# A gated mix of attention and ReLU-GLU on one core: new orders for the passes in the attention's rounds of three and four halves

## The chip, the cores and the metric

One core of one Trainium2 chip. The metric is device microseconds of one execution, the median of the runs shown. Below, "the profiled execution" is the one that left the trace.

## The reference, cut to what matters

x has 2048 rows (tokens) of 448 features. Two branches read it, and a gate of one number a token mixes them:

```
g = sigmoid((x * gate_w).sum(-1))
q, k, v = split(x @ wqkv)          # 16 heads of 28
p = softmax(q @ k.T * 28 ** -0.5)  # 2048 x 2048 a head
a = (p @ v) @ wo
gate, up = x @ W_gate, x @ W_up    # 1792 wide
h = gate * (gate > 0) * up
b = h @ W_down
out = g * a + (1 - g) * b
```

## The kernel before, in words

Everything is float32 outside. Where products need the precision, an operand is split in a high and a low float32r part, and a product is the sum of several passes: 11 matmuls (TERMS, L57) of 512 columns for one tile of q, k, gate or up.

A **first stage** (to about 125 us) makes q, k and v and starts on the attention. A **last stage** (from about 1090 us) is the output product and the down product of the other branch. Between them lie 32 **rounds**, and the change is in these. Each round works on eight key tiles of one head (128 keys against all 2048 queries), so a head takes two rounds. TensorE's order in a round is written out by hand, in a string with one letter for each piece of work (L43 to L48; the loop over the letters is L591 to L628):

- `s`, `scores` (L173): one matmul (L178) of a key tile against 512 queries, 114 rows deep, two of which bring in the queries' maxima. ScalarE takes its exp into P (L180). The result stands in one of **two** PSUM buffers `s` in turn, so a score must wait until the exp of the score two before it is done.
- `m`, `smax` (L144): two matmuls (L152) for the maxima of a head that comes later; VectorE reduces 128 x 1024 of them (L154). Two PSUM buffers `mx` in turn.
- `x`, `gu_mm` (L462): one of the 11 passes (L468) of one half, gate or up, of a tile of 128 of the other branch's hidden columns. When a gate half is full, ScalarE takes its relu (L481); after an up half VectorE multiplies (L484) and GpSimd sends the tile to HBM (L490). Two PSUM buffers `x` in turn.
- `h`: the last passes of the round's last two halves, 64 rows each, side by side.

After the string come the splits of the next weights (ScalarE L90, GpSimd L99) and `pv` (L496): 64 matmuls (L503) of P with V, which stand in one of the two `mx` buffers. Its result is copied by ScalarE (L507) after the first round of a head, and added by VectorE (L509) after the second.

Before the string `small_things` (L554) issues DMAs, and it does so again at the string's 17th `s`. In every second round, `smax_end` (L159) follows: TensorE transposes a head's maxima (L162), ScalarE copies them twice (L165, L166), VectorE subtracts (L96), and GpSimd sends two rows to Q (L169). Below a round is called odd when it begins with this, which also is when L507 stands ahead of it. Each engine works its instructions off in the program's order, so in an odd round the first exp of the string stands behind L507, L165 and L166 on ScalarE, and the first reduction behind the subtraction on VectorE.

Which strings run (L50, L52): FIRST once; then 28 rounds, of which 24 are LONG (three halves of gate and up) and four are WIDE (four halves; the 3rd, 6th, 9th and 18th of the 28); then LATE three times. Of the 28, the 1st, 3rd and so on are odd. A matmul of 512 columns is called a pass below: `s` and `x` are one, `m` is two.

A matmul is a weight load (PEld) and the stream (PE). A load runs beside the matmul ahead of it. The wait for a PSUM buffer is a wait of the load.

Of the kernel before, what the change touches and what calls it, by code (L numbers as in the profile page):

```python
# [41 lines left out]

FIRST = "s" * 12 + "mmlssxxxmsxsxuxmsxmsxsxmsxsxmsxsxmsxsxmsxsxmsxsxmsxsxmsx"  # L43

LONG = "mxsmsxxxxxsmsxsmsxxsmsxsmsxxsmxxsmsxsxxsmsxxsxsmxsxsmsxxsmsxsmsxxsmsxsxxsmsmxssh"
WIDE = "sxxmxmxxsxxmsxxsxsmxxssxmxmxsxxsxxsxsmsxxsmxssxxxsmsxxsxmsxmsxsxmsxsmxsxsxxsmsxxsmsmsxxsxsh"

LATE = "ssxxxssxxxssxxssxx" * 4 + "hh"  # L48

ROUNDS = [(FIRST, 2)] + ([(LONG, 3)] * 2 + [(WIDE, 4)]) * 2 + [(LONG, 3)] * 2  # L50

ROUNDS += ([(WIDE, 4)] + [(LONG, 3)] * 8) * 2 + [(LONG, 3)] * 2 + [(LATE, 4)] * 3  # L52
NP = 9
# [757 lines left out]
```

## Time and profile before

| | |
|---|---|
| median of 3 runs | 1297.71 us (1297.41 to 1298.08) |
| profiled execution, its own time | 1295.85 us |
| its span, first to last instruction | 1294.1 us |
| granted TensorE clock | 1.000 |
| busy: VectorE, ScalarE, GpSimd | 62%, 59%, 28% |
| first turned maxima in the 28 rounds | 166.2 us |
| first round of LATE | 1014.8 us |

In the profile a row of a timeline has the start, the length, the engine, the line of the kernel, what it writes and reads, and how many like it were merged; in brackets stand the idle time ahead of it and what ended that. The ends of matmuls are modelled; their starts are what can be compared. A row of the waits has who waited, for whom, the total in us, how often, and the longest.

### The profile page before, as it was taken

Reading aid. Unit: us, or ns where it says so; the run is one execution under the profiler, and the core shown is the slowest. Engines: PE = TensorE matmul, PEld = TensorE weight load, DVE = VectorE, ACT = ScalarE, POOL = GpSimd, SP = SyncE. Lnnn points to the kernel's source line nnn. Section 1 sums busy time; section 2 is a strip of 40 time slices with the busy share of each in tenths; the row PEclk is TensorE's granted clock in tenths of the full one; section 3 lists DMA queues with packets and bytes.
Section 4 is the critical chain, followed back from the end, with each engine's and each line's share of the span. In section 5 each row is a group of like instructions: output and inputs, shape, how many; then the busy total and the mean of one; then the engine's idle time right before and its main releaser. Section 6 shows DMA issues by size and latency. Waiting matters only on the chain.

```text
span 1294.1 us, 17710 instructions
## 1 busy us (share of the span) xinstructions
PE 1287.5 (99%) x6687; PEld 901.8 (70%) x6687; DVE 806.1 (62%) x834; ACT 767.0 (59%) x1402; POOL 365.8 (28%) x551
## 2 busy tenths in 40 slices
PE   9999999999999999999999999999999999999998
PEld 6888766666666666666666666666666656899997
DVE  6488766677677676777766667777777212663342
ACT  5212766666767677777776666767676865322121
POOL 3222132332313222222223332313132353641020
PEclk9999999999999999999999999999999999999999
DMA  9845524151426334141535142422341224644432
GB/s 322 284 162 229 155 75 103 60 124 55 117 63 182 76 81 96 52 103 45 139 108 119 50 111 66 109 69 79 71 142 38 82 91 142 198 136 148 134 110 78
DMA packets 53565, 148.87 MB, mean 115 GB/s; under 512 B 10024, under 2 KB 17128, under 8 KB 48872
## 3 DMA queue, kind: packets, MB, share of 16 engines
q1 hardware_dynamic: 36120, 98.34, 28.9%
q0 software_dynamic: 16928, 48.93, 10.5%
q8 instruction: 53, 0.87, 0.3%
q10 hardware_dynamic: 432, 0.46, 0.1%
q14 instruction: 32, 0.26, 0.1%
HBM read 102.06 MB, written 46.02 MB: 114 GB/s over the span
## 4 chain that ended last, share of the span: by engine, by line
PE 98%; ACT 0%; DMA 0%; SPq 0%; DVE 0%; issue 0%; ACTq 0%
PE gu L468 22%; PE sm L152 19%; PE po L503 17%; PE s L178 17%; PE acc L712 11%; PE qk L303 5%; PE v L321 3%; PE wo L668 3%; PE s L189 2%; DMA wr<-wq 0%; PE mt L162 0%; ACT WO L90 0%; SPq L253 0%; DVE W L96 0%; ACT V L191 0%
## 5 line engine op out<-in xcount | busy, mean ns | idle before, releaser
L154 DVE TENSOR_REDUCE mx<-sm 128x1 f32<-128x1024 f32 x512 | 614.4, 1221 | 106.1 <-PE sm L152 105.6
L180 ACT ACTIVATE P<-s 128x512 f32<-128x512 f32 x724 | 414.5, 597 | 161.8 <-PE s L178 123.0
L468 PE MATMUL gu<-X,wg 128*128 128x512 f32 (+1 forms) x1232 | 391.0, 400 | 0.2 <-ACT wg L90 0.2
L178 PE MATMUL s<-Q,K 114*128 114x512 f32 x932 | 367.6, 400 | 0.0
L152 PE MATMUL sm<-K,Q 112*128 112x512 f32 x1024 | 323.6, 397 | 0.0
L468 PEld LDWEIGHTS gu<-X,wg 128*128 128x128 f32 (+1 forms) x1232 | 226.6, 189 | 52.8 <-issue 8.8
L178 PEld LDWEIGHTS s<-Q,K 114*128 114x128 f32 x932 | 175.2, 188 | 88.9 <-ACT P L180 47.9
L152 PEld LDWEIGHTS sm<-K,Q 112*128 112x128 f32 x1024 | 192.1, 190 | 44.7 <-issue 10.1
L503 PE MATMUL po<-P,V 128*32 128x512 f32 x1600 | 181.0, 594 | 0.0
L490 POOL DMA_DIRECT2D h_d<-h x56 | 31.4, 560 | 518.7 <-DVE h L484 472.4
L99 POOL TENSOR_TENSOR wg<-wgr,wg 128x384 fp32r<-128x384 f32 x204 | 145.6, 731 | 8.1
L180 ACT ACTIVATE V<-s 128x512 f32<-128x512 f32 x208 | 119.5, 598 | 41.6 <-PE s L178 30.5
L712 PE MATMUL acc<-WD,hh 128*128 128x448 f32 x672 | 140.9, 368 | 0.0
L712 PEld LDWEIGHTS acc<-WD,hh 128*128 128x128 f32 x672 | 126.2, 188 | 12.8
L503 PEld LDWEIGHTS po<-P,V 128*32 128x32 f32 x1600 | 49.6, 110 | 111.2 <-issue 110.1
L90 ACT ACTIVATE hh<-hr 128x512 fp32r<-128x512 f32 x56 | 35.2, 631 | 119.3 <-PE acc L712 119.3
L96 DVE TENSOR_TENSOR hh<-hr,hh 128x512 fp32r<-128x512 f32 x56 | 46.1, 823 | 64.2 <-ACT hh L90 64.2
L303 PE MATMUL qk<-X,W 128*128 128x512 f32 x308 | 79.3, 398 | 0.3
L303 PEld LDWEIGHTS qk<-X,W 128*128 128x128 f32 x308 | 58.4, 190 | 14.9 <-ACT zt L326 0.5
L90 ACT ACTIVATE wg<-wgr 128x384 fp32r<-128x384 f32 x165 | 66.3, 491 | 2.3 <-PE gu L468 1.2
L509 DVE TENSOR_TENSOR os<-po,os 128x512 f32<-128x512 f32 x16 | 11.1, 691 | 88.8 <-PE po L503 88.8
L96 DVE TENSOR_TENSOR mh<-mr,mh 16x128 fp32r<-16x128 f32 x16 | 5.9, 366 | 91.3 <-ACT mh L166 91.3
(73 smaller groups left out, 756.6 us busy)
## 6 DMA issues: line engine op xcount, KB each, us to landing
wgr<-wgu SPq DMA_DIRECT2D x55, 512.0 KB
K<-qk_d SPq DMA_DIRECT2D x64, 224.0 KB
Q<-qk_d SPq DMA_DIRECT2D x64, 224.0 KB
h_d<-h POOLq DMA_DIRECT2D x56, 256.0 KB, 2.3
hr<-h_d SPq DMA_DIRECT2D x56, 256.0 KB
qk_d<-st POOLq DMA_DIRECT2D x21, 512.0 KB, 3.9
x_d<-X POOLq DMA_DIRECT2D x6, 1024.0 KB, 5.1
X<-x_d SPq DMA_DIRECT2D x24, 256.0 KB
```

The lines of the kernel that those rows point to most:

```text
L90: nc.scalar.activation(dst, src, AF.Copy)
L96: nc.vector.tensor_tensor(dst, src, f32(high), op=OP.subtract)
L99: nc.gpsimd.tensor_tensor(dst, src, f32(high), op=OP.subtract)
L152: nc.tensor.matmul(ps[:, c, :], Q[h][:GD, u * P:(u + 1) * P], K[h % 3][:GD, k0:k0 + TB], start=True, stop=True)
L154: nc.vector.tensor_reduce(MX[h][:, 2 * u + half:2 * u + half + 1], ps, axis=AX.XY, op=OP.max)
L178: nc.tensor.matmul(ps, K[h % 3][:GD + 2, kt * P:(kt + 1) * P], Q[h][:GD + 2, j * TB:(j + 1) * TB], start=True, stop=True)
L180: nc.scalar.activation(PT[i][:, j], ps, AF.Exp, scale=SCALE)
L303: nc.tensor.matmul(ps, W[:, a, c * P:(c + 1) * P], xf(tb, b), start=(n == 0), stop=(n == NT - 1))
L321: nc.tensor.matmul(ps[:, :VC], xf(tb, b)[:, t * P:(t + 1) * P], W[:, a, 2 * D:], start=(n == 0), stop=(n == NT - 1))
L468: nc.tensor.matmul(ps, WS[i][rows, s, a], xf(i // NF, b)[rows], start=(n == 0), stop=(n == NT - 1))
L503: nc.tensor.matmul(po[32 * j:32 * j + 32], V[:, h // 4 % 2, i % NK, h % 4], p[:, j], start=(i == i0), stop=(i == i0 + ni - 1))
L712: nc.tensor.matmul(ACC[i // NF][t][:, :D], HH[i][:, a, t * P:(t + 1) * P], WD[:, f, b], start=(f == 0 and n == 0), stop=(f == NF - 1 and n ...
```

## The change

The two strings LONG and WIDE are written anew. Both keep their letters: 32 `s`, 16 `m`, 31 `x` (WIDE: 42) and one `h`; only their order differs. The rest of the kernel is as it was.

```
-LONG = "mxsmsxxxxxsmsxsmsxxsmsxsmsxxsmxxsmsxsxxsmsxxsxsmxsxsmsxxsmsxsmsxxsmsxsxxsmsmxssh"
-WIDE = "sxxmxmxxsxxmsxxsxsmxxssxmxmxsxxsxxsxsmsxxsmxssxxxsmsxxsxmsxmsxsxmsxsmxsxsxxsmsxxsmsmsxxsxsh"
+LONG = "smsxmsxsxmsxsxmsxsmxsxsmxsxsxmsxsmxsxsxxxsmsmsxxsxmsxsxmsxsmxsxsmxsxsxmsxsmxxssh"
+WIDE = "xssmxxsxxsxxmssxmxsxxmssmxxsxsmxsxsmxsxsxxxxxxssmxxsxxmsxsmxsxsmxsxmsxsmxsxsmxsxxsmsxxsmxsh"
```

Counted in passes from the string's start, the first scores, the first maxima and the smallest distances are:

| | scores at | m at | smallest, score to next but one | smallest, m to next but one |
|---|---|---|---|---|
| LONG before | 3, 6, 12, 15, 17 | 0, 4, 13, 18 | 5 | 11 |
| LONG after | 0, 3, 7, 9, 13 | 1, 5, 11, 17 | 6 | 10 |
| WIDE before | 0, 10, 15, 18, 20 | 3, 6, 13, 21 | 5 | 9 |
| WIDE after | 1, 2, 7, 10, 15 | 3, 13, 18, 24 | 6 | 10 |

## The prediction

> **What bounds the kernel now.** I read the page first. TensorE works all the time and the chain that ended last runs through it.
>
> ```profile
> PE 1287.5 (99%) x6687; PEld 901.8 (70%) x6687; DVE 806.1 (62%) x834; ACT 767.0 (59%) x1402; POOL 365.8 (28%) x551
> ...
> PE 98%; ACT 0%; DMA 0%; SPq 0%; DVE 0%; issue 0%; ACTq 0%
> ```
>
> A busy PE may still place its matmuls further apart than it must. So the second view is the weight loads' waits between 166 and 1014.7 us, the 28 rounds whose orders change (24 LONG, 4 WIDE). A row gives the total us, the count and the longest wait.
>
> ```profile
> PEld s L178 <- ACT P L180: 47.4, 263, 0.2
> PEld s L178 <- ACT V L180: 13.8, 77, 0.2
> ...
> PEld po L503 <- DVE mx L154: 1.0, 4, 0.2
> ```
>
> The weights of a score wait 340 times for an exp; nothing waits for the maxima (m) except four short times at the products with V. Counting passes in the old strings (s and x one pass, m two) explains the number: in LONG 13 of the 30 scores with a score two before them in the round stand five passes behind it, in WIDE 7, and no score stands nearer. 24 x 13 + 4 x 7 = 340. Every five is late and no six is.
>
> The third view is the timeline inside one LONG round: start, length, engine.
>
> ```profile
> 446.15 0.40 PE L178 MATMUL s<-Q,K 114*128 114x512 f32 x1
> ...
> 446.58 2.49 ACT L180 ACTIVATE P<-s 128x512 f32<-128x512 f32 x4 [0.80 <-PE s L178]
> ...
> 446.86 0.39 PE L178 MATMUL s<-Q,K 114*128 114x512 f32 x1
> ...
> 447.09 0.39 PE L468 MATMUL gu<-X,wg 128*128 128x512 f32 x1
> 447.23 0.19 PEld L178 LDWEIGHTS s<-Q,K 114*128 114x128 f32 x1 [0.18 <-ACT P L180]
> 447.32 0.42 PE L178 MATMUL s<-Q,K 114*128 114x512 f32 x1
> ...
> 447.58 0.62 PE L152 MATMUL sm<-K,Q 112*128 112x512 f32 x2
> 447.94 0.19 PEld L178 LDWEIGHTS s<-Q,K 114*128 114x128 f32 x1 [0.17 <-ACT P L180]
> 448.04 0.40 PE L178 MATMUL s<-Q,K 114*128 114x512 f32 x1
> ...
> 448.28 0.62 PE L468 MATMUL gu<-X,wg 128*128 128x512 f32 x2
> ```
>
> Score at 446.15, exp at 446.58 (0.43 later), which lasts 0.60 and ends at 447.18; the load for the next score but one starts at 447.23, 0.05 later. So 1.08 us pass from a score to the load that it holds back, if ScalarE is free. The passes are 0.23 apart (446.86, 447.09, 447.32), and a load usually starts a whole pass ahead. This one starts 0.09 ahead; the next matmul comes 0.26 on, not 0.23. The load at 447.94 starts 0.10 ahead and costs 0.01. So some 0.10 ahead is free, what is missing is paid, and the idle 0.18 of a load costs about 0.03.
>
> Fourth, what all 340 cost. The mean lengths of the matmuls of these rounds, and the spread of the scores (shortest/median/longest):
>
> ```profile
> L178 PE MATMUL s<-Q,K 114*128 114x512 f32 x896 | 353.4, 400 | 0.0
> L468 PE MATMUL gu<-X,wg 128*128 128x512 f32 x912 | 304.7, 395 | 0.0
> L152 PE MATMUL sm<-K,Q 112*128 112x512 f32 x896 | 283.6, 398 | 0.0
> ...
> L178 PE MATMUL s<-Q,K x896: 389/396/501, 167.1 to 1007.0; 114*128 114x512 f32 x180
> ```
>
> A score's recorded length grows with the lateness (0.42 above, against 0.39). Mean less median is 4 ns, x 896 = 3.6 us. Against the gate-and-up matmuls it is 5 ns, 4.5 us.
>
> **The change part by part.** Nothing is added or taken out: each string keeps its 32 s, 16 m, its x and its h (31 x in LONG, 42 in WIDE), and with them all loads, splits and DMAs. Only places move. The DMAs that SP issues at the 17th score move by under five passes (1.2 us) in a round of 23 us; no transfer is waited for there in the rows of loads.
>
> *Removed.* In the new strings the smallest distance of a score to the next but one is six. Six passes are 1.39 us; the chain takes 1.08, so the load may start 0.31 ahead, where 0.10 is enough: 0.21 to spare. All 340 late loads should go. Counting: of a LONG's 13, some 7 cost 0.02 to 0.03 and three 0.01, about 0.18; 24 x 0.18 + 4 x 0.1 = 4.7 us. The means said 3.6 and 4.5. I take **4.6**; the ends are 3.6 and 5.2.
>
> Two scores two passes apart, which the new LONG has twelve times, queue on ScalarE. The nearest row is two scores one pass apart:
>
> ```profile
> 402.80 0.65 PE L178 MATMUL s<-Q,K 114*128 114x512 f32 x2
> ...
> 403.23 1.09 ACT L180 ACTIVATE P<-s 128x512 f32<-128x512 f32 x2 [0.33 <-PE s L178]
> ```
>
> Two exps end in 1.09, so the second starts 0.49 after the first. For scores at pass 0 and 2 the second exp starts at 0.92 instead of 0.89: 0.03 of the 0.21 to spare. A relu stands behind the 11th x, at pass 34, in about every second LONG; with it the exp of the score at pass 37 starts 0.10 late, and the load for pass 43 still starts 0.2 ahead. I cost both at nothing; a miss is a rival below.
>
> *Added.* The front of a round. In the odd rounds a head's maxima are turned by a transpose (14 in the window, in 12 LONG and 2 WIDE), and ScalarE and VectorE have three small pieces of work ahead of the first exp and the first maximum. The old WIDE begins with a score, as the new LONG does. Its front:
>
> ```profile
> L162 PE MATMUL mt<-ident,m 128*16 128x128 f32 x14 | 3.9, 277 | 0.0
> ...
> 410.81 0.28 PE L162 MATMUL mt<-ident,m 128*16 128x128 f32 x1
> 410.84 0.48 PE L178 MATMUL s<-Q,K 114*128 114x512 f32 x1
> 410.94 0.60 ACT L507 ACTIVATE os<-po 128x512 f32<-128x512 f32 x1 [3.89 <-PE po L503]
> 411.16 0.63 PE L468 MATMUL gu<-X,wg 128*128 128x512 f32 x2
> ...
> 411.44 0.25 ACT L165 ACTIVATE mr<-mt 16x128 f32<-16x128 f32 x1
> ...
> 411.72 0.31 ACT L166 ACTIVATE mh<-mr 16x128 fp32r<-16x128 f32 x1
> ...
> 411.94 0.57 ACT L180 ACTIVATE P<-s 128x512 f32<-128x512 f32 x1
> ```
>
> The first exp starts 1.13 after the transpose and ends at 1.70, though its score was ready at 0.5. There the old WIDE has its third score at pass 15, far off. The new strings have it at pass 7. Pass 1 is at 0.35, so pass 7 is at 0.35 + 6 x 0.233 = 1.75; the load is released at 1.70 + 0.05 = 1.75, just when the matmul should start. What that costs shows at the round's first matmul, whose load also starts with it: 410.84 to 411.16 is 0.32 where 0.23 is usual. **0.10 in each of 14 rounds.** The second exp follows 0.50 behind the first (410.94 to 411.44 for two that queue), ends at 2.23 and releases at 2.28. In the new LONG its score stands at pass 9, 2.21 + 0.10 = 2.31: the load starts 0.03 ahead where some 0.10 are needed to cost nothing, another **0.06 in 12 rounds**. In WIDE it is pass 10 and free.
>
> Then the maxima. The old LONG's odd front on VectorE, the spread of the small subtraction and the reduction's mean:
>
> ```profile
> 473.19 0.28 PE L162 MATMUL mt<-ident,m 128*16 128x128 f32 x1
> ...
> 474.44 0.28 DVE L96 TENSOR_TENSOR mh<-mr,mh 16x128 fp32r<-16x128 f32 x1 [6.21 <-ACT mh L166]
> ...
> 474.65 3.60 DVE L154 TENSOR_REDUCE mx<-sm 128x1 f32<-128x1024 f32 x3
> ...
> L96 DVE TENSOR_TENSOR mh<-mr,mh x16: 268/331/529, 110.0 to 1016.0; 16x128 fp32r<-16x128 f32 x16
> ...
> L154 DVE TENSOR_REDUCE mx<-sm 128x1 f32<-128x1024 f32 x512 | 614.4, 1221 | 106.1 <-PE sm L152 105.6
> ```
>
> The subtraction starts 1.25 after the transpose; with 0.28 the first reduction starts at 1.46 and ends at 2.67, with 0.53 at 2.92. The third m needs that buffer. It moves from pass 13 (3.15) to pass 11: 0.35 + 10 x 0.233 + 0.16 of waits already = 2.84, and costs nothing if its load starts by 2.74. Released at 2.72 it is free, at 2.97 it costs 0.23. The median of 0.33 gives 0.03; I take 0.05, ends 0 and 0.23. Behind it the m are five to seven passes apart against 1.21 us (5.2 passes) for a reduction, and the wait is not handed on. In even rounds there is no turn:
>
> ```profile
> 443.25 0.73 PE L152 MATMUL sm<-K,Q 112*128 112x512 f32 x2
> 443.39 0.69 DVE L509 TENSOR_TENSOR os<-po,os 128x512 f32<-128x512 f32 x1 [5.65 <-PE po L503]
> ```
>
> VectorE's addition ends 0.83 after the round's start, when the first maximum of the new order is not yet ready (pass 2 at 0.58, and 0.43 more). The first exp can start at about 0.5. Both leave room.
>
> Sum of the new waits: 14 x 0.10 + 12 x (0.06 + 0.05) = **2.7 us**; ends 1.4 (only the third score) and 14 x 0.10 + 12 x (0.07 + 0.23) = 5.0.
>
> The Trainium skill, "SBUF — State Buffer", section "Who interferes with whom", says that a VectorE instruction with two SBUF inputs contends with a GpSimd instruction that reads SBUF. The subtraction is such an instruction, and its 268 to 529 ns agree; which rounds GpSimd's splits will meet decides between the ends already used.
>
> *Sum.* -4.6 + 2.7 = **-1.9 us** on a span of 1294.1. The profiled execution took 1295.85, so 1293.95; the median of the three runs is 1297.71, 1.86 above it, so **1295.8 us**.
>
> **Rivals.**
> - *The fronts are free.* If the first exp of an odd round did not wait behind the three small pieces, only -4.6 is left: 1293.1. The row at 411.94 speaks against it. 18%.
> - *Slower: the pairs.* ScalarE may give two queued exps 0.70 apart, not 0.50. For a pair at pass 0 and 2 the second then ends at 0.43 + 0.70 + 0.60 = 1.73 and releases at 1.78; its next but one stands at 8 passes, 1.86, and 0.08 ahead costs 0.025. Twelve pairs x 24 rounds are 7.2 us: -4.6 + 2.7 + 7.2 = +5.3, 1303.0. It decides from 0.68 apart on. For it speaks the row of four exps in 2.49 (0.63 apart on average), but those scores came three, two and three passes apart; against it the two in 1.09. 7%.
> - *It doesn't do what it says:* the longer spacing of late scores belongs to something else, stays, and only the new waits come: +2.7, 1300.4. Against it: exactly the 340 fives. 8%.
> - *All idle of the loads is price.* Then 340 waits of 0.18, less the usual 0.04 each, leave: 61.2 - 13.6 = 47.6, less 2.7 of new waits, 1252.8. The row 447.32 to 447.58 shows 0.03 for a wait of 0.18, so 1%. The Trainium skill, "TensorE: Matmul & The Clock Gate", section "The mechanism", says that a weight load overlaps running matmuls only when its row group differs, by which the loads would stand bare on the path; the trace differs, its loads of 114 rows lie wholly beside matmuls.
>
> **How the numbers follow.** The forecast holds the other 66%, from 1294.3 (5.2 removed, 1.8 added) to 1299.1 (3.6 removed, 5.0 added), mostly near the middle. With 18% near 1293.1 and the far rivals left out, the range is 1292.9 to 1298.4. A measurement of this kernel tells about 0.2%, 2.6 us. Faster than 1295.1: 18 + 1 and 13 of the forecast, 32%. Slower than 1300.3: 7 and some 5 of the third rival, 12%. Between: 56%.
>
> **What would show it.** The waits of scores for exps fall from 340 to some 26 to 40, all in the first 2.5 us of odd rounds, at 0.2 us and more each. The scores' mean length falls to about 396. Even LONG rounds get shorter by about 0.18, odd ones stay. Waits of scores for exps spread over the round would prove the pairs right; waits for the reductions beyond the third m would mean that VectorE binds, and the forecast is wrong.

## The result, and the profile after

| | before | after |
|---|---|---|
| median, 8 runs each | 1297.76 us (1297.41 to 1298.08) | 1294.22 us (1293.42 to 1294.71) |
| ratio | | 0.9972, 95% interval 0.9964 to 0.9981 |
| profiled execution, and its span | 1295.85, 1294.1 us | 1294.10, 1292.3 us |
| once more, on another chip | 1296.14 us (27 runs) | 1293.64 us (11 runs), ratio 0.9981 (0.9972 to 0.9990) |

The forecast was 1295.8 us, 1.9 less than before. The spans of the two traces differ by 1.8, the medians by 3.5 here and by 2.5 on another chip. So there are two questions: do the forecast's terms stand behind the 1.8, and where does the rest come from?

The head of the page of after, and the waits of its weight loads between 166 and 1014.7 us:

```profile
span 1292.3 us, 17710 instructions
```

```profile
PEld po L503 <- DVE mx L154: 5.9, 24, 0.2
PEld s L178 <- ACT P L180: 4.6, 20, 0.3
PEld sm L152 <- DVE mx L154: 3.9, 13, 0.7
PEld s L178 <- ACT V L180: 1.4, 6, 0.3
```

The 340 waits of scores are 26 now: two in each of 12 odd LONG fronts and one in each of two odd WIDE fronts. Thirteen waits of m have come. The 24 of the products are a change of name only: a product's first load idled about as long before the change, then put down to its issue, and the products follow the `h` at the same distance (0.42 to 0.43 us, rows below).

The lengths of the scores' matmuls say the same, in the mean (400 before) and in shortest/median/longest (389/396/501):

```profile
L178 PE MATMUL s<-Q,K 114*128 114x512 f32 x896 | 350.2, 398 | 0.0
...
L178 PE MATMUL s<-Q,K x896: 388/393/504, 166.6 to 1005.3; 114*128 114x512 f32 x180
```

An even LONG round, from its first matmul to the first product. In before the one that begins at 443.25 (a row of the prediction) ends so, and below it is the same round of after:

```profile
465.76 0.49 PE L468 MATMUL gu<-X,wg 64*128 64x512 f32 x2
466.18 1.06 PE L503 MATMUL po<-P,V 128*32 128x512 f32 x8
```

```profile
443.56 0.50 PE L178 MATMUL s<-Q,K 114*128 114x512 f32 x1
...
465.83 0.50 PE L468 MATMUL gu<-X,wg 64*128 64x512 f32 x2
466.26 1.07 PE L503 MATMUL po<-P,V 128*32 128x512 f32 x8
```

22.93 us has become 22.70. An odd LONG has hardly gained (22.96 in before, 22.92 here); this is its front in after, and its first product (the old front stands in the prediction):

```profile
473.27 0.28 PE L162 MATMUL mt<-ident,m 128*16 128x128 f32 x1
...
473.41 0.60 ACT L507 ACTIVATE os<-po 128x512 f32<-128x512 f32 x1 [5.00 <-PE po L503]
...
474.40 2.25 ACT L180 ACTIVATE P<-s 128x512 f32<-128x512 f32 x4
474.52 0.28 DVE L96 TENSOR_TENSOR mh<-mr,mh 16x128 fp32r<-16x128 f32 x1 [6.81 <-ACT mh L166]
...
475.02 0.19 PEld L178 LDWEIGHTS s<-Q,K 114*128 114x128 f32 x1 [0.28 <-ACT P L180]
475.02 0.50 PE L178 MATMUL s<-Q,K 114*128 114x512 f32 x1
...
475.36 0.39 PE L468 MATMUL gu<-X,wg 128*128 128x512 f32 x1
475.50 0.19 PEld L178 LDWEIGHTS s<-Q,K 114*128 114x128 f32 x1 [0.18 <-ACT P L180]
475.59 0.41 PE L178 MATMUL s<-Q,K 114*128 114x512 f32 x1
...
475.84 0.40 PE L468 MATMUL gu<-X,wg 128*128 128x512 f32 x1
475.99 0.30 PEld L152 LDWEIGHTS sm<-K,Q 112*128 112x128 f32 x2 [0.20 <-DVE mx L154]
476.07 0.65 PE L152 MATMUL sm<-K,Q 112*128 112x512 f32 x2
...
496.19 1.06 PE L503 MATMUL po<-P,V 128*32 128x512 f32 x8
```

The first exp starts 1.13 after the transpose. The third score's load is let go 1.75 after it, exactly when its matmul should start, and the next matmul comes 0.34 on instead of 0.23. The fourth score starts its load 0.09 ahead and costs 0.02; the third m starts its load 0.08 ahead and costs 0.03.

One wait was not foreseen, in the round at 380.8 us:

```profile
392.53 0.63 PE L152 MATMUL sm<-K,Q 112*128 112x512 f32 x2
...
393.92 0.25 DVE L517 RECIPROCAL rs<-ls 128x16 f32<-128x16 f32 x1 [1.68 <-DMA ls<-os]
394.09 3.42 DVE L154 TENSOR_REDUCE mx<-sm 128x1 f32<-128x1024 f32 x3
...
394.62 0.39 PE L468 MATMUL gu<-X,wg 128*128 128x512 f32 x1
395.30 0.30 PEld L152 LDWEIGHTS sm<-K,Q 112*128 112x128 f32 x2 [0.72 <-DVE mx L154]
395.31 0.73 PE L152 MATMUL sm<-K,Q 112*128 112x512 f32 x2 [0.29 <-DVE mx L154]
```

VectorE works in the program's order. It has come to the reciprocal of the row sums (issued at the string's 17th score) and waits 1.68 us for their transfer; the reduction of the maxima that TensorE made at 392.53 stands behind it, and then TensorE waits for that reduction: 0.69 us pass from 394.62 to 395.31 instead of 0.23, and 0.1 more is lost behind it.

### The profile page after: what moved, and what is told of

The parts are those of the page before. It is cut to its first block, busy times and chain, and to the rows that moved or that the text cites. A ratio compares the mean times of both kernels' runs of the same rounds, so it can differ in the third digit from the quotient of the medians.

```text
span 1292.3 us, 17710 instructions
## 1 busy us (share of the span) xinstructions
PE 1285.5 (99%) x6687; PEld 923.7 (71%) x6687; DVE 808.6 (63%) x834; ACT 749.2 (58%) x1402; POOL 366.9 (28%) x551
## 4 chain that ended last, share of the span: by engine, by line
PE 94%; issue 2%; DMA 1%; POOL 1%; ACT 1%; DVE 0%; SPq 0%; ACTq 0%; POOLq 0%
PE gu L468 21%; PE sm L152 18%; PE po L503 16%; PE s L178 16%; PE acc L712 11%; PE qk L303 5%; PE v L321 3%; PE wo L668 3%; PE s L189 2%; DMA ls<-os 1%; POOL wg L99 1%; DMA wr<-wq 0%; PE mt L162 0%; ACT wg L90 0%; ACT WO L90 0%
## 5 line engine op out<-in xcount | busy, mean ns | idle before, releaser
L180 ACT ACTIVATE P<-s 128x512 f32<-128x512 f32 x724 | 401.3, 596 | 174.3 <-PE s L178 164.2
L468 PE MATMUL gu<-X,wg 128*128 128x512 f32 (+1 forms) x1232 | 422.3, 401 | 0.2 <-ACT wg L90 0.2
L99 POOL TENSOR_TENSOR wg<-wgr,wg 128x384 fp32r<-128x384 f32 x204 | 146.3, 735 | 8.1
L180 ACT ACTIVATE V<-s 128x512 f32<-128x512 f32 x208 | 115.1, 596 | 45.6 <-PE s L178 43.4
L90 ACT ACTIVATE hh<-hr 128x512 fp32r<-128x512 f32 x56 | 35.2, 631 | 119.5 <-PE acc L712 119.5
L96 DVE TENSOR_TENSOR hh<-hr,hh 128x512 fp32r<-128x512 f32 x56 | 46.1, 824 | 64.2 <-ACT hh L90 64.2
L90 ACT ACTIVATE wg<-wgr 128x384 fp32r<-128x384 f32 x165 | 66.3, 490 | 3.8 <-DMA wgr<-wgu 2.6
L96 DVE TENSOR_TENSOR mh<-mr,mh 16x128 fp32r<-16x128 f32 x16 | 5.9, 368 | 91.5 <-ACT mh L166 91.5
```

Of the source, the lines that this page charges most:

```text
L90: nc.scalar.activation(dst, src, AF.Copy)
L96: nc.vector.tensor_tensor(dst, src, f32(high), op=OP.subtract)
L99: nc.gpsimd.tensor_tensor(dst, src, f32(high), op=OP.subtract)
L180: nc.scalar.activation(PT[i][:, j], ps, AF.Exp, scale=SCALE)
L468: nc.tensor.matmul(ps, WS[i][rows, s, a], xf(i // NF, b)[rows], start=(n == 0), stop=(n == NT - 1))
```

## The experiments

My theory, from the prediction: late weight loads of the scores go, and shorter waits come at the odd rounds' fronts, because ScalarE and VectorE do three small pieces of work in order ahead of the first exp and the first reduction. The rivals: the gain between the medians comes from elsewhere; the fronts cost nothing; any rewriting does it.

**The kernel before once more, LONG alone, WIDE alone** (one chip).

```diff
 e1: no edit
 e2: LONG as after, WIDE as before
 e3: LONG as before, WIDE as after
```

> The kernel before, once more, to learn what an execution of it does beside the one in the first trace. The spans of the two traces differ by 1.8 us (1294.1 and 1292.3), the medians by 3.5 (1297.76 and 1294.22). Theory A: the string's price is 1.8 and the traced execution of before was a lucky one; the other 1.9 us are waits for transfers that most executions of before have and the traced one hasn't (the row sums' transfer ahead of the reciprocal, L517, is the candidate: in the trace of after it costs 0.6 in one round). Then this trace has a span near 1296 and shows waits of the reductions or scores that are not in the first one. Theory B: the trace itself changes the time; then this trace again has a span near 1294 and an execution time near 1295.9, while the timed ones stay at 1297.7.

> Only LONG is new, WIDE as before. If the price lies with the scores five passes apart, LONG had 24 x 13 of the 340, and its 12 odd fronts have nearly all the new waits: the 340 late loads fall to 28 of the old kind in WIDE and some 24 at the odd fronts, and the time lies within 0.5 us of the kernel with both strings (1294.2). If most of the gain between the medians came from elsewhere, it stays near 1296 to 1297.

> Only WIDE is new, LONG as before. By the sum: 4 x 0.10 less, 2 x 0.10 more at the odd fronts, so 0.2 us less than before, not to be told from it, and 312 late loads left. If the change works by something that any rewriting brings (the state of the transfers, where the executions fall), it would be as much faster as both strings, some 2 to 3.5 us.

Before had a median of 1297.68 us on this chip, one of its 23 executions at 1295.91. Once more it took 1297.80 (ratio 0.9999, 0.9990 to 1.0008) and its traced execution again 1295.86, with the same span of 1294.1: theory A's waits are not there, and so far it looked like B. LONG alone took 1293.69 (0.9969, 0.9957 to 0.9980), all of the gain. WIDE alone took 1297.64 (1.0000, 0.9991 to 1.0009), nothing, as the sum has it. So it isn't any rewriting. Their waits, LONG alone first:

```profile
PEld s L178 <- ACT P L180: 8.2, 41, 0.3
...
PEld s L178 <- ACT V L180: 2.3, 11, 0.3
```

```profile
PEld s L178 <- ACT P L180: 43.8, 242, 0.3
PEld s L178 <- ACT V L180: 12.9, 72, 0.2
```

52 are 28 old ones in WIDE and 24 at the odd fronts; 314 are 312 in LONG and two at WIDE's odd fronts. Both are the counted numbers.

The traced execution of WIDE alone took 1298.25 us, so a traced execution can lie at the upper time too. It shows where such an execution loses time. Below are two stretches of the first stage, whose program is the same in both kernels, first in before and then in WIDE alone. A row has the stretch and its length, then for TensorE, its loads, VectorE, ScalarE and GpSimd the busy us and the number of instructions, then the granted clock, the transfers' share and GB/s:

```profile
5.00:11.00 6.00, 5.80 (x19) 3.85 (x18) 5.73 (x13) 5.34 (x13) 1.78 (x8) 1.00 1.04 366
11.00:14.40 3.40, 3.40 (x16) 2.75 (x16) 3.36 (x5) 2.80 (x4) 0.88 (x1) 1.00 0.76 246
```

```profile
5.00:11.00 6.00, 4.78 (x13) 2.03 (x12) 4.74 (x10) 4.28 (x12) 1.78 (x8) 1.00 0.96 344
11.00:14.40 3.40, 3.33 (x9) 2.50 (x9) 3.31 (x6) 2.37 (x3) 0.89 (x1) 0.50 0.62 193
```

From 5 to 11 us TensorE idles 1.2 us in WIDE alone and 0.2 in before; then its granted clock in WIDE alone is one half for 3.4 us, in which lie 9 matmuls instead of 16. The first of the 28 rounds begins at 168.9 instead of 166.2, 2.6 us later, which is more than the 1.8 between the two times. The idle time begins with a transfer: ScalarE waits 0.84 us for a part of the weights (until 7.06), and TensorE 0.90 us for ScalarE (until 8.40). LONG alone and the trace of e10 (below) idle 0.4 and 0.3 us in the same six and keep the full clock. So the idle time is the likely cause of the half clock, but no run sets it by itself. The Trainium skill, "TensorE: Matmul & The Clock Gate", section "Part 1: The HAM clock gate (the "warmup" mystery)", says that the clock falls to half after an idle window of about 3.4 us, and that these windows run freely and don't begin with the kernel. The length of the stretch at half clock (10.98 to 14.39 us) agrees; a whole idle window did not come ahead of it here, only 1.2 us in six.

**More warming, and after once more** (another chip).

```diff
-WARM = 11
+WARM = 16      # e8: in before; e9: in after; e10: after, no edit
```

> The kernel before with 16 instead of 11 warming matmuls ahead of the first stage. Executions of before come at two times, near 1295.9 and near 1297.7; the trace of WIDE alone, which took 1298.25, has its first round start 2.6 us later than the trace of before (168.9 against 166.2), a granted clock of one half from 10.98 to 14.39 us, and matmuls at 0.43 there. If the upper time is that window of half clock, brought by the idle time of TensorE between the warming matmuls and the first products, more warming fills it: all executions near 1296 (some tenths more where the warming itself delays the first product). If the two times come from elsewhere, both are still seen.

> The kernel after with 16 warming matmuls. It has shown no window of half clock after the start so far, so the time stays within 0.5 us of after (1294.2). The difference to before with 16 warming matmuls on the same chip is then the price of the strings alone: 1.8 us by the two traces (span 1294.1 and 1292.3), against 3.5 between the medians. If the change is worth 3.5 by itself, the difference is 3.5.

> The kernel after once more, beside before on the same chip. Where before lies at 1295.9 to 1296.1 the difference is 1.8; where it lies at 1297.7, and after has no window of half clock, it is 3.5.

On this chip before had all 27 executions between 1295.83 and 1296.48 (median 1296.14), so the upper time wasn't there to be cured, and e8 with 1296.18 (ratio 1.0000, 0.9991 to 1.0009) tells nothing of it. That the half clock makes the upper time rests on one trace. What brings the upper time stays open: on the chip of e1 to e4 nearly every execution of before had it and all of WIDE alone, none of LONG alone; of the 19 of after at most one had it (1295.30, on this chip); and the traced executions of before were at the lower time even where the others were not. But the pair without it is clean: 1293.64 for after (0.9981, 0.9972 to 0.9990), and 1293.56 with more warming: 2.5 and 2.6 us less. Of the 3.5 us of the first comparison about 1.0 to 1.8 are then the upper time of before, not the price of the strings. The trace of e10 has a span of 1291.7, 0.6 less than the first of after, and no late transfer in any of the 28 rounds.

**The small things two scores later.**

```diff
-                if ns == 4 * NB:
+                if ns == 4 * NB + 2 * (order in (LONG, WIDE)):
                     small_things(i0 // 4 + 1)
```

> Both new strings, but the small pieces of work that stand at the 17th score of a round stand at its 19th score in LONG and WIDE, which is pass 51 of LONG as it was pass 50 before the change (after the change pass 45). If the reciprocal (L517) stood too early for its transfer, its waits for it in the middle rounds, 3.9 us in four rounds in the trace of after, go, and with them the wait of 0.6 us in the round at 380.8: about 0.6 us less than after, 1293.6. If the transfer was late by itself, the wait stays.

On the chip of e1 to e3 it took 1293.45 us beside before's 1297.68 (0.9967, 0.9955 to 0.9979), 0.8 less than after had beside 1297.76, but only 0.2 less than LONG alone on the same chip. Counted in passes from the string's start, the 17th score of LONG stands at pass 53 before the change and at 49 after it, and the edit puts the small things at pass 55; the 50, 45 and 51 above are miscounted, but the direction is right. The reciprocal's waits, the row of after and the row of this one (total and count). Two of them lie behind the 28 rounds in both, 6.7 us in after and all 5.9 here; so the 28 rounds have three waits of 3.1 us in after and none here:

```profile
  DMA ls<-os: 9.8, 5
```

```profile
  DMA ls<-os: 5.9, 2
```

The edit takes the waits away that the earlier place brought. Their lengths differ from execution to execution: the traces of after, e9, e10 and e12 (the last kernel below) have 13 of them in their 28 rounds. The ten of under 1 us lengthen no round. The three of 1.58 to 1.73 us lengthen theirs by 0.5 to 0.6: the round at 380.8 in after, at 803.9 in e9, at 860.7 in e12. So the wait is real, its price between 0 and 0.6 an execution, and the timed difference too small to settle it.

**Free fronts.** First the copy alone, then the copy and the scaling, then both with the small things later (e5, e6, e7; the chip of e8 to e10, where after took 1293.64; before at 1296.13, 15 runs).

```diff
 e5, e6, e7:
-            nc.scalar.activation(OS[h], po, AF.Copy)
+            nc.vector.tensor_copy(OS[h], po)
 e6, e7:
-        if h and q == 2:
-            normalise(h - 1)
...
+        if i0 and i0 % NK == 0:
+            normalise(i0 // NK - 1)
         pv(i0, ni)
```

> Both new strings; the copy of the products of a head's first round (L507) is done by VectorE instead of ScalarE. If the third score of an odd round waits for ScalarE's queue, the first exp starts at about 0.8 us instead of 1.13 after the transpose, and the waits of the scores at pass 7 and 9 go (0.10 + 0.015 in each odd LONG, 0.10 in WIDE as the trace of after has them, 1.6 us in all). But VectorE then does the copy (0.69) and behind it the scaling of the head before (L528, 0.68), which so far ran beside the products and now stands behind the copy: the small subtraction ends near 1.8 and the first reduction near 3.0 in all odd rounds, so the third m waits about 0.3 in each of 12, 3.6 us, against 1.1 in after. Sum: +0.9, about 1295.1. If VectorE's queue is of no weight, 1292.6.

> As the last, and the scaling (L528 with its four transfers) stands ahead of the products of the odd round's beginning instead of behind them, so that VectorE does it beside the products as before. Then the copy ends at 0.83, the subtraction starts when ScalarE is through with its two small copies, near 0.95, the first reduction starts at 1.3 and ends at 2.5, and neither the scores nor the third m wait: after less 2.3 us, about 1291.9. If the waits at the odd fronts are not what the trace says, it stays at 1294.

> As the last, and the pieces of the 17th score at the 19th. All waits that the trace of after shows in the 28 rounds should be gone: the sum of the two gains, 2.3 + 0.6, so about 1291.3. If the late transfer is chance, it equals the last within 0.3.

The copy alone: 1294.46 us (0.9989, 0.9980 to 0.9998), 0.8 more than after on this chip where 0.9 were expected. No score waits any more, and the third m waits instead. Its VectorE, behind a transpose at 472.45:

```profile
472.59 0.69 DVE L507 COPY os<-po 128x512 f32<-128x512 f32 x1 [6.29 <-PE po L503]
473.20 0.68 DVE L528 TENSOR_TENSOR os<-os,rb 128x512 f32<-128x512 f32 x1
473.80 0.27 DVE L96 TENSOR_TENSOR mh<-mr,mh 16x128 fp32r<-16x128 f32 x1
474.00 2.34 DVE L154 TENSOR_REDUCE mx<-sm 128x1 f32<-128x1024 f32 x2
```

```profile
PEld sm L152 <- DVE mx L154: 6.5, 11, 0.8
```

The first reduction starts 1.55 after the transpose (1.46 in after) and 6.5 us of waits stand at m. With the scaling ahead of the products: 1289.27 us (0.9948, 0.9936 to 0.9961), 6.9 less than before and well under both kernels. Behind its transpose at 471.52:

```profile
471.65 0.69 DVE L507 COPY os<-po 128x512 f32<-128x512 f32 x1 [5.69 <-PE po L503]
...
472.34 1.05 ACT L180 ACTIVATE P<-s 128x512 f32<-128x512 f32 x2
...
472.47 0.28 DVE L96 TENSOR_TENSOR mh<-mr,mh 16x128 fp32r<-16x128 f32 x1
...
472.68 3.47 DVE L154 TENSOR_REDUCE mx<-sm 128x1 f32<-128x1024 f32 x3
...
494.24 1.06 PE L503 MATMUL po<-P,V 128*32 128x512 f32 x8
```

```profile
PEld sm L152 <- DVE mx L154: 0.8, 4, 0.2
```

The first exp starts at 0.82 instead of 1.13, and no score waits. The odd LONG is 22.72 long, as the even one. It gave 4.4 against after, more than the 2.3 expected. By the traces of e10 and e6 the 28 rounds gave 3.1, since the odd fronts had cost more than I had read (below), and the three LATE rounds 1.0, from a wait that I hadn't counted: in the last of them the exps stood on ScalarE behind the same copy and behind two splits of the output weights (L90, 1.78 us) that come after it in the program. Before, and this kernel at the same place:

```profile
1066.29 0.63 PE L468 MATMUL gu<-X,wg 128*128 128x512 f32 x2
1067.70 0.72 PE L189 MATMUL s<-Q,K 114*128 114x512 f32 x2 [0.78 <-ACT V L191]
```

```profile
1062.62 0.63 PE L468 MATMUL gu<-X,wg 128*128 128x512 f32 x2
1063.10 0.66 PE L189 MATMUL s<-Q,K 114*128 114x512 f32 x2
```

1.41 against 0.48 from the one row to the next. All three together took 1289.42 (0.9948, 0.9936 to 0.9961), no more: the late transfer was no part of this gain.

**The old strings with free fronts** (another chip again; before at 1297.62, 15 runs). This is meant to take the new waits out of the comparison and to leave the removed term alone. The edit is that of e6, e11 in before, e12 in after.

> The old strings with the copy on VectorE and the scaling ahead of the products. The old strings had no waits at the odd fronts, so by the sum only the wait of 1.2 us that ScalarE's copy made in the last round of LATE goes: about 1.0 us less than before, near 1295.1 where before is at 1296.1, and the 340 late loads stay. If the free fronts are worth their 4.9 us with any strings, 1291.2.

> The new strings with free fronts once more, on the same chip as the last. The difference of the two is the removed term alone, without new waits: 4.6 us by the forecast (ends 3.6 and 5.2); by the rounds' lengths in the traces (LONG from 22.93 to 22.71, WIDE from 25.43 to 25.32) 24 x 0.22 + 4 x 0.11 = 5.7. So 1289.3 against 1295.1.

The old strings took 1296.72 (0.9992, 0.9983 to 1.0001), 0.9 less than before. That is not LATE's wait alone, since before lies at its upper time here and this kernel does not: its trace has the full clock and its first round at 166.7 us, where WIDE alone had 168.9.

```profile
11.00:14.40 3.40, 3.40 (x16) 2.78 (x15) 3.37 (x4) 2.97 (x4) 0.89 (x1) 1.00 0.70 236
```

Against the trace of before, which is at the lower time too (span 1294.1), its span of 1295.0 is 0.9 longer: the LATE rounds are 1.1 shorter, as expected, but the 28 rounds are 1.5 longer together and begin 0.4 later. The old LONG is 23.02 us here (22.93 in before); why, stays open. The free fronts are worth nothing with the old strings, so the 1291.2 is out. Their loads wait as before:

```profile
PEld s L178 <- ACT P L180: 47.0, 263, 0.2
PEld s L178 <- ACT V L180: 13.7, 77, 0.2
```

The new strings took 1289.92 (0.9940, 0.9926 to 0.9953): 6.8 less than the old ones here. That isn't the removed term alone, since 1.5 of it are the longer rounds of the old strings in this pair.

## Why the prediction was right, step by step

- **The bound** (late loads of scores, all of them the fives): right. 340 went, and in each mixed kernel the counted number stayed.
- **Removed, 4.6 us (3.6 to 5.2):** right in kind, too small, and outside its own ends. By the rounds' lengths of before and of the kernel with free fronts it is 24 x 0.22 + 4 x 0.11 = 5.7 us (5.8 added up round by round). The difference of 6.8 between e11 and e12 is no measure of it, for the reason above. The price was the mis-sized part: I took it from a mean of 4 ns a score and from starts printed to 0.01, both too coarse for 340 prices of about 0.02. The trace of before has these prices (away from a round's last passes): sorted by how far the late load starts ahead of its matmul, the next matmul comes 0.259 us on (0.08 ahead, 116 loads), 0.252 (0.09, 98 loads), 0.237 (0.10, 66 loads) or 0.23 as behind a load that isn't late (0.11 and 0.12, 60 loads), which makes 5.3 us.
- **The pairs two apart, at nothing:** right; no score waits outside the fronts. That rival is dead, and so is the one that the loads' whole idle time is price: it fell by 55 us (61.2 to 6.0), the time by 2 to 3 (3.5 where before was at its upper time).
- **Added, 2.7 us (1.4 to 5.0):** mechanism and places right, the third score's 0.10 was 0.11, the fourth's 0.06 was 0.02. As lengths, an odd LONG of after is 22.91 in seven rounds and 23.05 to 23.16 in five, where a free one has 22.72: 7 x 0.19 + 4 x 0.33 + 0.44 + 2 x 0.12 for WIDE = 3.3. The five are those whose subtraction was slow (0.42 to 0.53, each time beside one of GpSimd's splits, L99; 0.28 in the seven); there the third m cost 0.14 to 0.25 more, near the upper end (0.23), where I had taken 0.05 on average. The rival that the fronts are free is dead: freeing them gave 3 us and more.
- **Nothing is waited for at the 17th score:** wrong. The prediction read the waits of TensorE's loads and SP's transfers, and not VectorE's reciprocal, which is issued there too and stands in line ahead of reductions. It came four passes earlier in LONG (pass 49 for 53) and six in WIDE (54 for 60, where the prediction had said under five). It cost 0.6 in the traced execution and nothing in another.
- **The sum:** -5.7 + 3.3 + 0.6 = -1.8, as the two traces differ, and -2.4 without the late transfer, near the 2.5 between the medians 1296.14 and 1293.64. That the forecast -1.9 meets the first is partly luck: both terms were a fifth too small, so that their difference held, and a term of 0.6 was left out. The agreement of the traces is rough too: the 28 rounds of after are 2.1 shorter together, and begin 0.4 later, in a stage that the change doesn't touch.
- **The median is 1.86 above the profiled execution:** wrong as a step. Before has two times, 1.8 us apart; its trace was at the lower and its median at the upper. That step carried the upper time over to after, put the forecast at 1295.8, and is most of the 1.6 us by which after, at 1294.2, came out below it. The size of the change was forecast as within 0.2% with 56%; it is 0.19% against the lower time of before, 0.28% against the upper.

## What to carry to other kernels

Count, in an order written by hand, how many passes lie between an instruction and the one that needs its buffer back; if the count alone reproduces the number of waits in the trace, each wait's price can be summed and an order without them written. Then check the same distances where the pattern begins, behind whatever the other engines still have in line, and for every small instruction that hangs on a letter of the order: here moving one copy and one scaling gave more than the new order had (4.4 against 2.5 us on one chip), and with the old order it gained nothing in the rounds. And when a profiled execution lies outside the spread of the timed ones, find out what it lacks before adding the difference to a forecast.

## What the runs showed of the hardware that was not expected

- In the traced execution of WIDE alone, TensorE's granted clock fell to 0.50 for 3.4 us, 11 us after its start, and 1.2 us of idle time lay between 5 and 11 us; its rounds began 2.6 us later than those of before. That the idle time was the cause is not shown.
- A score's weight load that starts 0.11 us or more ahead of its matmul costs nothing in the trace of before, though a load mostly starts a whole pass (0.23) ahead. One that starts 0.10 ahead costs 0.005, 0.09 ahead 0.02, 0.08 ahead 0.03; one that starts with its matmul costs 0.10 to 0.11 (in the trace of after).
- The small subtraction on VectorE (16 x 128, L96) took 0.28 us in seven odd LONG rounds of after, and 0.42 to 0.53 in the five in which a split on GpSimd (L99) lay over it for 0.28 us or more (0.04 at most in the seven).
